# Folding two modulation vectors, and four places in the order of a one-core transformer block

## The chip, the cores and the metric

The kernel runs on one core of a Trainium2 chip. The metric is the device time of one execution in microseconds; lower is better. Profiles come from the hardware profiler, from one execution each.

The engines are named as the profile names them: PE is TensorE's matrix multiplication and PEld its weight load, DVE is VectorE, ACT is ScalarE, POOL is GpSimd, SP is SyncE, which here issues plain DMAs. GpSimd issues the DMAs that add to what they find at their target.

## The reference

One block over `x` of 2048 tokens by 448 channels, all in float32: a linear attention with 16 heads of 28 channels, then a mixer that multiplies across the tokens. Six modulation vectors of 448 values come from the conditioning vector `c`.

```python
mod = (_silu(c) @ w_mod)                 # 6 x 448: sa, ca, ga, sb, cb, gb
h = _layernorm(x) * (1 + ca) + sa
qkv = h @ wqkv
phi = lambda t: where(t > 0, t + 1, exp(t)) + 1e-6
kv, z = phi(k)^T v per head, sum of phi(k) over tokens
o = (phi(q) kv) / (phi(q) z + 1e-6)
x = x + ga * (o @ wo)
h = _layernorm(x) * (1 + cb) + sb
u = gelu(h^T @ w1 + b1)                  # contraction over 2048 tokens, 1792 wide
x = x + gb * (u @ w2 + b2)^T
```

In the code the vectors have numbers: 0 is `sa`, 1 `ca`, 2 `ga`, 3 `sb`, 4 `cb`, 5 `gb`.

## The kernel before, in words

**Two parts for one number.** Matrix products run in the fast 32-bit form, which rounds its operands. So most operands are cut into a high part (a rounded copy, made by ScalarE) and a low part (the rest), and one product becomes three matmuls: high by high, high by low, low by high. `split` (line 78) does it with ScalarE and VectorE. Some low parts are made the other way: ScalarE writes minus the high part, and a DMA of GpSimd adds the full number to it (`w_low_dma`, line 217; `low`, line 399; the second branch of `a_pk_parts`, line 424). A projection of one tile of 128 tokens is 11 matmuls, over four chunks of the 448 channels; the last chunk has 64 channels and holds its high and low part in one tile, so it needs two.

**The stages.** First the modulation vectors 0 and 1 and tile 0. Then a loop over the tiles, one pass for each `t` from 3 to 15 (line 594): TensorE projects the keys of tile `t` (`kp`), transposes tile `t + 1` (`tp`), and adds the outer product of tile `t - 3` (`cacc`, from the parts of phi(k), `pkh` and `pkl`, and of the normalised rows, `xh` and `xl`). The other engines normalise tile `t + 2`, make phi(k) of tile `t`, cut phi(k) of tile `t - 1` into its parts, take the statistics of tile `t + 3` and so on. After the loop the key-value matrices are formed, then come the queries, the residual and the second layer norm (a loop from line 855), the first mixer product (`up`, to line 1163) and the second (`y`, to line 1183), which uses Strassen's seven products on 2 x 2 blocks.

**What sets the order.** Every engine runs its instructions in the order in which the program writes them down; there is no scheduler. So the place of a call in the loop's body is its place in that engine's queue, and an instruction that waits holds up all behind it on its engine. Waits between engines and for buffers are put in from the data each instruction uses. Most tiles share one pool of 76 buffers (`slots`).

**The places the change touches.**

- `project` (line 343) writes down the 11 matmuls of a projection. With `late_low` it sorts them: high parts by high weights first, then low parts, then the low weights, then chunk 3. Only the queries of tile index 1, the second tile, are projected so (line 582). Of their weights' low parts, `wl0_0` comes by DMA (line 541), the others from VectorE.
- Vectors 2 to 5 are summed off the critical start: `mod_part` multiplies 112 rows of `w_mod` by `silu(c)` and adds them up over four pieces on VectorE, so that one tile of 112 rows by 448 is left, whose column sums are the vector. `mod_split` (line 191) cuts it into two tiles, `mod_sum2` (line 196) sums the columns with a matrix of ones: one matmul for the high part (line 199), one for the low part (line 200). `mod_out` copies the result. For vector 2 the four parts are in passes 5 to 8, the split at the end of pass 9, the sum and the copy in pass 10; in passes 11 to 14 the four row groups of `wo` are multiplied by it (line 611). For vector 4 the parts are in passes 11 to 14 (`MOD_AT`), split and sum after the loop (lines 670 and 686).
- `PK_LOW` lists the tiles whose low part of phi(k) VectorE makes, beside `DVE_LOW`. For the others it is ScalarE and GpSimd's DMA.
- `mult7` (line 1014) writes the matmuls of the second mixer product. For the very last product the last `LAST` of 7 row blocks are set aside for `last7` (line 1038), which puts them into a bank of their own, `yl`, with three matmuls of 224 columns for each; VectorE then adds the two halves of the main bank and the closing bank to `x`, and the result is stored.

Of the kernel before, what the change touches and what calls it, by code (L numbers as in the profile page):

```python
# [11 lines left out]
ALU = mybir.AluOpType  # L12
# [3 lines left out]
S, D, F = 2048, 448, 1792  # L16
NT = S // P
NF = F // P
G = 112
# [7 lines left out]
Q_EARLY = (3, 4)  # L27
QLATE = 2
MOD_ACT = (0, 1)
PK_LOW = (9,)  # L30
DVE_LOW = (0, 1, 13, 14, 15)
AHEAD = 8
LAG = 5
LAST = 2
PRE2 = {16: (1, 0), 12: (1, 1), 8: (1, 2), 3: (4, 3), 1: (4, 4)}
MOD_AT = {11: [(4, 0)], 12: [(4, 1)], 13: [(4, 2)], 14: [(4, 3)], 15: [(3, 0), (3, 1)]}
QS = {0: 2, 4: 2}
WARM = 9
ACT_STATS = ()
PRE = 9  # L40
# [7 lines left out]
def block_kernel(ctx: ExitStack, tc: tile.TileContext, x, wqkv, wo, w1, b1, w2, b2, c, wmod, out):  # L48
    nc = tc.nc
# [22 lines left out]
    def moving(new, name, dt=F32R, parts=P):  # L72
        return new(name, dt=dt, parts=parts, w=512)[:, 16:16 + D]

    def bank(name):
        return psum.tile([P, 512], F32, name=name, tag="bank")

    def split(full, hi, lo):
        nc.scalar.activation(hi, full, AF.Copy)  # L79
        nc.vector.tensor_sub(lo, full, hi.bitcast(F32))  # L80
# [4 lines left out]
    ones_r = cst.tile([P, P], F32R, name="ones_r")  # L85
# [55 lines left out]
    def keep_warm(n):  # L141
        for i in range(n):
            nc.tensor.matmul(warm[:, :P], ones, ones, start=True, stop=True)
# [3 lines left out]
    nc.tensor.transpose(ct, c_sb, ident[:4, :4])  # L147
    keep_warm(WARM)

# [7 lines left out]
    mods, macc, part = {}, {}, {}  # L157
# [17 lines left out]
    def mod_part(j, k):  # L175
        if k == 0:
            macc[j] = (tslot if j == 5 else slot)(f"acc{j}", parts=G)
            if j == 5:
                nc.scalar.activation(macc[j], wm[j, 0], AF.Copy, scale=sc[:, 0:1])
            else:  # L180
                nc.vector.tensor_scalar_mul(macc[j], wm[j, 0], sc[:, 0:1])
        else:
            nc.vector.scalar_tensor_tensor(macc[j], wm[j, k], sc[:, k:k + 1], macc[j], op0=ALU.mult, op1=ALU.add)
# [4 lines left out]
        return ps  # L188


    def mod_split(j):
        acc = macc.pop(j)
        macc[j] = (moving(slot, f"mh{j}", parts=G), moving(slot, f"ml{j}", parts=G))
        split(acc, *macc[j])

    def mod_sum2(j):
        ps = bank(f"modp{j}")
        hi, lo = macc.pop(j)
        nc.tensor.matmul(ps[:, :D], ones_r[:G, :], hi, start=True, stop=False)
        nc.tensor.matmul(ps[:, :D], ones_r[:G, :], lo, start=False, stop=True)  # L200
        return ps
# [103 lines left out]
    def a_norm_a(t):  # L305
        h = slot(f"h{t}", 512)
        nc.vector.scalar_tensor_tensor(h[:, :D], X[t], st[t][0], mods[1],
                                       op0=ALU.add if t in ACT_STATS else ALU.subtract, op1=ALU.mult)
        hs[t] = h

    def a_norm_b(t, sa=None):
        h = hs[t]
        nc.vector.scalar_tensor_tensor(h[:, :D], h[:, :D], st.pop(t)[1], mods[0] if sa is None else sa,
                                       op0=ALU.mult, op1=ALU.add)

    def a_dup(t):
        nc.scalar.activation(hs[t][:, D:], hs[t][:, 384:D], AF.Copy)
# [3 lines left out]
    def a_transpose(t):  # L321
        h = hs[t]
        tps[t] = bank(f"tp{t}")
        for ch in range(4):
            nc.tensor.transpose(tps[t][:, ch * P:(ch + 1) * P], h[:, ch * P:(ch + 1) * P], ident)  # L325

    def a_split(t):
        hh = slot(f"hh{t}", 512, F32R)
        hl = slot(f"hl{t}", 512, F32R)
        split(tps.pop(t), hh, hl)  # L330
        heads[t] = (hh, hl)
# [11 lines left out]
    def project(t, j, name, late_low=False):  # L343
        hh, hl = heads[t]
        ps = bank(f"{name}{t}")
        o = ps[:, :D]
        todo = []
        for ch in range(4):
            a, b = (hh, ch, Whi[j, ch]), (hl, ch, Whi[j, ch])
            todo += [a, b] if ch == 3 else [a, (hh, ch, Wlo[j, ch]), b]  # L350
        if late_low:
            ws = [Wlo[j, ch] for ch in range(3)]
            key = lambda m: 3 if m[1] == 3 else 2 if any(m[2] is w for w in ws) else 0 if m[0] is hh else 1
            todo.sort(key=key)
        for n, (a, ch, b) in enumerate(todo):
            nc.tensor.matmul(o, a[:, ch * P:(ch + 1) * P], b, start=(n == 0), stop=(n == 10))  # L356
        return o
# [3 lines left out]
    def a_exp(t, ps):  # L361
        eks[t] = (slot(f"ek{t}"), slot(f"rk{t}"))
        nc.scalar.activation(eks[t][0], ps, AF.Exp)
        nc.scalar.activation(eks[t][1], ps, AF.Relu)
# [20 lines left out]
    def a_q(t):  # L385
        qps[t] = project(t, 0, "qp")
        del heads[t]
# [33 lines left out]
    def a_pk(t, ps):  # L421
        pkf[t] = phi_k(t, ps, tslot if t < 2 else slot)

    def a_pk_parts(t):
        pk = pkf.pop(t)
        hi, lo = moving(slot, f"pkh{t}"), moving(slot, f"pkl{t}")
        nc.scalar.activation(hi, pk, AF.Copy, bias=1e-6)
        if t in DVE_LOW or t in PK_LOW:
            nc.vector.scalar_tensor_tensor(lo, pk, 1e-6, hi.bitcast(F32), op0=ALU.add, op1=ALU.subtract)
# [14 lines left out]
    def a_outer(t):  # L444
        if not cacc:
            cacc.extend(bank(f"cacc{ch}") for ch in range(4))
        xh, xl = xss.pop(t)
        kh, kl = pks.pop(t)
        for ch in range(4):
            s = slice(ch * P, (ch + 1) * P)  # L450
            todo = [(xh, kh), (xh, kl)] + ([(xl, kh)] if ch < 3 else [])
            for i, (a, b) in enumerate(todo):
                nc.tensor.matmul(cacc[ch][:, :D], a[:, s], b, start=(t == 0 and i == 0),  # L453
                                 stop=(t == NT - 1 and i == len(todo) - 1))
# [137 lines left out]
    wo_sb = []  # L592
    late = [t for t in range(KV_LAG, NT) if t not in Q_EARLY]
    for t in range(3, NT):
        kp = project(t, 1, "kp")
        if t + 1 < NT:
            a_transpose(t + 1)
        a_outer(t - KV_LAG)
        if t in Q_EARLY:
            a_q(t)  # L600
        if t == 10:
            mp = mod_sum2(2)
        if t + 1 < NT:
            a_split(t + 1)
        if t + 2 < NT:
            a_norm_a(t + 2)

        for j, i in MOD_AT.get(t, ()):
            mod_part(j, i)
        if 11 <= t < 15:  # L610
            nc.vector.tensor_mul(wo_sb[t - 11], wo_sb[t - 11], mods[2][:G])
        a_exp(t, kp)
        if t + 2 < NT:
            a_norm_b(t + 2)
        a_pk(t, kp)
        a_phi_q()
        a_pk_parts(t - 1)
        if t + 3 < NT:
            a_stats(t + 3)
        if t + 2 < NT:  # L620
            a_dup(t + 2)
        if t == 3:
            a_high(3)
            a_high(4)
        if t + 2 < NT:
            a_high(t + 2)
        if t == 10:
            mod_out(2, mp)
        if t + 4 < NT:
            load_x(t + 4)  # L630
        if 5 <= t < 9:
            mod_part(2, t - 5)
        if t == 9:
            mod_split(2)
        if 5 <= t <= 5 + QLATE:
            phi_q_sum(t - 5)
        if t in (10, 11):
            load_mod(14 - t)
        if t == 4:
            for g in range(4):  # L640
                w = tslot(f"wo{g}", parts=G)
                nc.sync.dma_start(w, wo[g * G:(g + 1) * G, :])
                wo_sb.append(w)
            load_qkv(2, tslot)
            b1c = cst.tile([P, NF], F32, name="b1c")
            nc.sync.dma_start(b1c, b1.rearrange("(k p) -> p k", p=P))
            b2c = cst.tile([P, NT], F32, name="b2c")
            nc.sync.dma_start(b2c, b2.rearrange("(k p) -> p k", p=P))
        load_to(PRE_LOAD.get(t, 0))
# [38 lines left out]
    for ch in range(4):  # L688
        for g in range(4):
            s = slice(g * G, (g + 1) * G)  # L690
            nc.tensor.matmul(kvb[:G, s], raw_w[2, ch][:, s], csum[ch][:, s], start=(ch == 0 and g == 0),  # L691
                             stop=(ch == 3), skip_group_check=True)
# [162 lines left out]
    for i in range(NT + LAG):  # L855
# [6 lines left out]
        if 0 <= i - 1 < NT:  # L862
            b_out(i - 1)
        nq = min(len(late), QS.get(i, 1))
        for _ in range(nq):
            a_q(late.pop(0))
        t = i - LAG
# [146 lines left out]
    def mult7(q, m, r0, r1):  # L1014
# [6 lines left out]
        for r in range(r0, r1):  # L1021
            (h, l), i = hilo[q, m][r // 4], r % 4
            w, wh = uops[b, r]
            s = slice(i * P, (i + 1) * P)
            if (q, m) == (NP - 1, 6) and r >= PAIRS - LAST:
                last.append((h[:, s], l[:, s], w))
                continue
            nc.tensor.matmul(ps[:, :D], h[:, s], w, start=opens and r == r0, stop=False, skip_group_check=True)  # L1028
            nc.tensor.matmul(ps[:, :HD], l[:, s], wh, start=False,  # L1029
                             stop=closes and r == PAIRS - 1 - (LAST if (q, m) == (NP - 1, 6) else 0),  # L1030
                             skip_group_check=True)
# [6 lines left out]
    def last7():  # L1038
        x = X[NT - 1][:, :HD]
        ps = bank("yl")[:, :HD]  # L1040
        for i, (h, l, w) in enumerate(last):
            for n, (a, b) in enumerate(((h, w[:, :HD]), (h, w[:, HD:]), (l, w[:, :HD]))):
                nc.tensor.matmul(ps, a, b, start=i + n == 0, stop=n == 2 and i == LAST - 1)
        for s in (acc2[NP - 1, 0][:, :HD], acc2[NP - 1, 0][:, HD:D], ps):
# [97 lines left out]
    for o0, n in W1G[1:]:  # L1142
# [5 lines left out]
        for r in range(first, NT):  # L1148
# [4 lines left out]
            if xleft and k % 2:  # L1153
                t = xleft.pop(0)
# [11 lines left out]
    for q, m, r0, r1 in order:  # L1166
        if jobs:
            jobs.pop(0)()
        while xleft:
            t = xleft.pop(0)  # L1170
# [41 lines left out]
```

## Time and profile before

| | |
|---|---|
| median of 3 runs | 440.61 us (440.5 to 441.14) |
| the profiled execution | 440.77 us |
| its span, first to last instruction | 439.1 us |
| granted TensorE clock | 1.000 |
| busy: DVE | 365.1 us (83%) |
| busy: ACT | 266.9 us (61%) |
| busy: POOL | 119.3 us (27%) |

Times in the profile count from the span's start. Busy times are the union of an engine's instructions. Matmuls are pipelined: the rows give each some 0.36 us for 448 columns, but the next one starts 0.20 us later, so their starts are what to compare. In the chain of work that ended last each line is start, length, and engine with tile and line; in a timeline a row is start, length, engine, line, operation, tiles, shapes and count, and in brackets how long the engine was idle before it and what ended that. Weight loads (PEld) run ahead of the matmuls; a matmul that must wait for its stationary operand shows as an idle PEld.

### The profile page before, as it was taken

The numbers are of one execution on the slowest core, as the hardware profiler recorded it, in microseconds if no ns is written. First come the engines' busy times: TensorE is split into PE (matmuls) and PEld (weight loads), VectorE is DVE, ScalarE is ACT, GpSimd is POOL, SyncE is SP. The second block draws the span as 40 slices with busy tenths as digits, with TensorE's granted clock in tenths as the row PEclk, the third lists the DMA queues.
The fourth block names the chain that finished last, engine by engine and source line by source line (L and its number), as shares of the span: only waits on it lengthen the run. The fifth ranks groups of instructions, "written<-read, shape, count | busy, mean of one in ns | idle before, by whom it ended". The sixth has DMA issues, their size and how long they took to land.

```text
span 439.1 us, 7288 instructions
## 1 busy us (share of the span) xinstructions
PE 433.9 (99%) x2394; PEld 402.4 (92%) x2394; DVE 365.1 (83%) x792; ACT 266.9 (61%) x570; POOL 119.3 (27%) x196
## 2 busy tenths in 40 slices
PE   8999999999999999999999999999999999999996
PEld 7689999999899999999999999999999999999996
DVE  5996898988898999997469586439999998898894
ACT  3778877655657777776766254236675555655550
POOL 2205775520024455664300000010112230231110
PEclk9999999999999999999999999999999999999999
DMA  8987999993441224222427546476667977977531
GB/s 233 303 213 117 181 197 230 221 258 102 138 100 26 47 47 123 50 50 60 132 69 237 177 143 186 131 194 187 151 143 191 177 172 176 188 161 208 75 52 34
DMA packets 65022, 64.51 MB, mean 147 GB/s; under 512 B 8472, under 2 KB 56792, under 8 KB 64984
## 3 DMA queue, kind: packets, MB, share of 16 engines
q1 hardware_dynamic: 54608, 47.62, 36.8%
q0 software_dynamic: 10368, 16.42, 23.8%
q8 instruction: 19, 0.31, 0.3%
q14 instruction: 19, 0.16, 0.1%
q10 hardware_dynamic: 8, 0.00, 0.0%
HBM read 41.88 MB, written 7.34 MB: 112 GB/s over the span
## 4 chain that ended last, share of the span: by engine, by line
PE 95%; DMA 3%; DVE 1%; ACT 0%; issue 0%; SPq 0%; DVEq 0%
PE y L1028 19%; PE up L829 10%; PE up L828 10%; PE up L830 10%; PE y L1029 9%; PE op L778 8%; PE cacc L453 8%; PE qp L356 7%; PE kp L356 7%; DMA wl<-wr 2%; PE tq L758 2%; PE tp L325 1%; DMA wm<-in_w_mod_dram 1%; PE kvb L691 1%; PE wp L846 1%; PE colp L475 0%
## 5 line engine op out<-in xcount | busy, mean ns | idle before, releaser
L829 PE MATMUL up<-h2l,ph 128*128 128x448 f32 x224 | 81.3, 363 | 0.0
L828 PE MATMUL up<-h2h,ph 128*128 128x448 f32 x224 | 81.2, 362 | 0.0
L830 PE MATMUL up<-h2h,pl 128*128 128x448 f32 x224 | 80.7, 360 | 0.0
L988 POOL DMA_DIRECT2D a<-a x16 | 14.1, 948 | 145.5 <-DMA a<-in_B_w_dram 97.8
L828 PEld LDWEIGHTS up<-h2h,ph 128*128 128x128 f32 x224 | 42.0, 188 | 3.3
L830 PEld LDWEIGHTS up<-h2h,pl 128*128 128x128 f32 x224 | 41.9, 187 | 3.0
L829 PEld LDWEIGHTS up<-h2l,ph 128*128 128x128 f32 x224 | 42.0, 188 | 2.1
L80 DVE TENSOR_TENSOR pl<-pr,ph 128x512 fp32r<-128x512 f32 x48 | 32.3, 686 | 11.5 <-ACT ph L79 8.6
L79 ACT ACTIVATE ph<-pr 128x512 fp32r<-128x512 f32 x48 | 29.1, 627 | 17.8 <-PE up L829 7.4
L1050 ACT ACTIVATE cc<-y 128x448 f32<-128x448 f32 x24 | 13.0, 544 | 22.9 <-PE y L1029 22.9
L453 PE MATMUL cacc<-pkh,xh 128*128 128x448 f32 x64 | 24.3, 379 | 0.0
L453 PE MATMUL cacc<-pkl,xh 128*128 128x448 f32 x64 | 23.2, 363 | 0.0
L778 PE MATMUL op<-oh,pth 128*128 128x448 f32 x60 | 23.0, 383 | 0.0
L1071 POOL DMA_DIRECT2D out_dram<-yt x14 | 12.9, 921 | 34.9 <-DVE yt L1057 25.4
L778 PE MATMUL op<-oh,ptl 128*128 128x448 f32 x60 | 21.7, 362 | 0.0
L356 PE MATMUL qp<-wh,hh 128*128 128x448 f32 x60 | 21.6, 365 | 0.0
L356 PE MATMUL qp<-wh,hl 128*128 128x448 f32 x60 | 21.4, 362 | 0.0
L356 PE MATMUL kp<-wh,hl 128*128 128x448 f32 x56 | 20.3, 363 | 0.0
L356 PE MATMUL kp<-wh,hh 128*128 128x448 f32 x56 | 20.2, 362 | 0.0
L736 POOL TENSOR_SCALAR den<-den 128x16 f32<-128x16 f32 x16 | 8.6, 536 | 39.2 <-DVE den L733 39.1
L763 ACT ACTIVATE pth<-tq 128x512 fp32r<-128x512 f32 (+1 forms) x16 | 9.6, 599 | 15.7 <-PE tq L758 15.6
L302 POOL TENSOR_TENSOR rs<-ve,mhalf 128x1 f32<-128x1 f32 x16 | 13.9, 869 | 18.8 <-DVE ve L300 18.5
(234 smaller groups left out, 1356.9 us busy)
## 6 DMA issues: line engine op xcount, KB each, us to landing
pr<-in_B_w_dram SPq DMA_DIRECT2D x56, 256.0 KB, 2.9
a<-in_B_w_dram SPq DMA_DIRECT2D x32, 256.0 KB, 4.3
a<-in_B_w_dram SPq DMA_DIRECT2D x32, 192.0 KB, 4.2
wm<-in_w_mod_dram SPq DMA_DIRECT2D x24, 196.0 KB, 4.9
x<-in_A_x_dram SPq DMA_DIRECT2D x16, 224.0 KB, 4.0
out_dram<-x SPq DMA_DIRECT2D x14, 224.0 KB, 2.0
out_dram<-yt POOLq DMA_DIRECT2D x14, 224.0 KB, 4.5
pk<-pk POOLq DMA_DIRECT2D x12, 224.0 KB, 4.7
```

The costliest lines, as they stand in the source:

```text
L79: nc.scalar.activation(hi, full, AF.Copy)
L80: nc.vector.tensor_sub(lo, full, hi.bitcast(F32))
L302: nc.gpsimd.tensor_tensor(rs, ve, mhalf[:, 0:1], op=ALU.pow)
L356: nc.tensor.matmul(o, a[:, ch * P:(ch + 1) * P], b, start=(n == 0), stop=(n == 10))
L453: nc.tensor.matmul(cacc[ch][:, :D], a[:, s], b, start=(t == 0 and i == 0), stop=(t == NT - 1 and i == len(todo) - 1))
L778: nc.tensor.matmul(opb[t][:, :D], a[:, g * P:(g + 1) * P], b, start=(n == 0), stop=(n == len(todo) - 1))
L828: nc.tensor.matmul(ps[:, :D], hi[:, sl], mh, start=first, stop=False)
L829: nc.tensor.matmul(ps[:, :D], hi[:, sl], ml, start=False, stop=False)
L830: nc.tensor.matmul(ps[:, :D], lo[:, sl], mh, start=False, stop=last)
L988: nc.gpsimd.dma_start(w, a, accum_op=ALU.add)
L1028: nc.tensor.matmul(ps[:, :D], h[:, s], w, start=opens and r == r0, stop=False, skip_group_check=True)
L1029: nc.tensor.matmul(ps[:, :HD], l[:, s], wh, start=False, stop=closes and r == PAIRS - 1 - (LAST if (q, m) == (NP - 1, 6) else 0), skip_gro ...
```

## The change

Five edits.

1. Vectors 2 and 4 are folded. When the 112-row tile is complete, a DMA of GpSimd with add puts rows 64 to 111 onto rows 0 to 47 of the same tile (`fold`). The split then takes 64 rows, and writes the high part to rows 0 to 63 and the low part to rows 64 to 127 of one tile, so that one matmul with 128 rows of ones sums both.
2. To make room for the fold of vector 2, it is issued at the end of pass 8, the split moves to the end of pass 10, sum and copy to pass 11, and the multiplications of `wo` to passes 12 to 15. The fold of vector 4 is issued in pass 14, right after its last part, ahead of that pass's other work on GpSimd.
3. In the late order of the second tile's queries, the product with `wl0_0` stands last, behind the other two low parts and chunk 3.
4. Tile 7's low part of phi(k) is made by VectorE.
5. `LAST` is 3 instead of 2.

```diff
-PK_LOW = (9,)
+PK_LOW = (7, 9)
-LAST = 2
+LAST = 3
+FOLDED = (2, 4)
...
+    def fold(j):
+        nc.gpsimd.dma_start(macc[j][:G - 64], macc[j][64:], accum_op=ALU.add)
+
     def mod_split(j):
         acc = macc.pop(j)
+        if j in FOLDED:
+            macc[j] = moving(slot, f"mb{j}")
+            split(acc[:64], macc[j][:64], macc[j][64:])
+            return
         macc[j] = (moving(slot, f"mh{j}", parts=G), moving(slot, f"ml{j}", parts=G))
...
     def mod_sum2(j):
         ps = bank(f"modp{j}")
+        if j in FOLDED:
+            nc.tensor.matmul(ps[:, :D], ones_r, macc.pop(j), start=True, stop=True)
+            return ps
...
-            key = lambda m: 3 if m[1] == 3 else 2 if any(m[2] is w for w in ws) else 0 if m[0] is hh else 1
+            key = lambda m: 3 if m[1] == 3 else 4 if m[2] is ws[0] else 2 if any(m[2] is w for w in ws) else 0 if m[0] is hh else 1
...
-        if t == 10:
+        if t == 11:
             mp = mod_sum2(2)
...
-        if 11 <= t < 15:
-            nc.vector.tensor_mul(wo_sb[t - 11], wo_sb[t - 11], mods[2][:G])
+        if t == 14:
+            fold(4)
+        if 12 <= t < 16:
+            nc.vector.tensor_mul(wo_sb[t - 12], wo_sb[t - 12], mods[2][:G])
...
-        if t == 10:
+        if t == 11:
             mod_out(2, mp)
...
         if 5 <= t < 9:
             mod_part(2, t - 5)
-        if t == 9:
+        if t == 8:
+            fold(2)
+        if t == 10:
             mod_split(2)
```

## The prediction

> **What bounds the kernel now.** I read the page first, then the chain of work that ended last, then TensorE's and its weight loads' timeline around each place that the diff touches.
>
> ```profile
> span 439.1 us, 7288 instructions
> PE 95%; DMA 3%; DVE 1%; ACT 0%; issue 0%; SPq 0%; DVEq 0%
> ...
> 17.43 8.12 DMA wl<-wr
> 25.60 3.48 PE qp L356 x16
> ```
>
> The chain is TensorE for 95% of 439.1 us. The only long piece of another kind behind the first microseconds is the DMA of `wl0_0`, 8.12 us, which ends at 25.55; TensorE takes up at 25.60 and is the chain from there to the last adds. So a change pays here in two coins only: matmuls that are no longer there, and holes in TensorE's row. Work on other engines costs nothing until it makes such a hole. The profiled execution took 440.77 us (its span and 1.67 around it), 0.16 over the median of the runs, 440.61. Some 0.2% (0.88 us) is about what a measurement of this kernel can tell from no change.
>
> **Part 1: the low part of the query weights last.** The query projection of tile index 1 (the second tile) waits for `wl0_0`, the one low part that comes by DMA.
>
> ```profile
> 24.75 0.77 PE L356 MATMUL qp<-wh,hl 128*128 128x448 f32 x3
> 25.60 0.88 PE L356 MATMUL qp<-wl,hh 128*128 128x448 f32 x3
> 26.31 0.36 PE L356 MATMUL qp<-wh,hh 128*128 128x448 f32 x1
> 26.51 0.36 PE L356 MATMUL qp<-wh,hl 128*128 128x448 f32 x1
> ...
> 25.60 0.50 PEld L356 LDWEIGHTS qp<-wl,hh 128*128 128x128 f32 x3 [0.45 <-DMA wl<-wr]
> ...
> 22.87 0.62 DVE L213 TENSOR_TENSOR wl<-wr,wh 128x448 fp32r<-128x448 f32 x1
> ```
>
> Undisturbed, matmuls start 0.20 apart (26.31, 26.51). Three from 24.75 would hand over at 25.35; the next starts at 25.60: 0.25 lost. From there three should take 0.60, but the next follows at 26.31: 0.11 more while the row restarts. That is 0.36. In the new order the two low parts that VectorE makes come next, then the two products of chunk 3, then `wl0_0`: four matmuls, 0.80, sooner than they would wait. VectorE's last low part ends at 23.49 and the one of chunk 3 follows it directly, so those four find their data. `wl0_0` is then wanted at 25.35 + 0.80 = 26.15, its weights some 0.2 before, 25.95; it lands at 25.55. Margin 0.4. Gain 0.36; bounds 0 (the DMA lands 0.8 later than here) and 0.36. Nothing is issued differently. What is late next: nothing near, as every matmul behind it runs at its 0.20.
>
> **Part 2: the two folded vectors.**
>
> ```profile
> 72.38 0.20 PE modp L199
> 72.58 0.21 PE modp L200
> ...
> 108.22 0.20 PE modp L200
> ```
>
> Each sum is now two matmuls of 112 rows; folded, it is one of 128 rows. One piece of 0.21 and one of 0.20 leave the chain: 0.41. That 128 rows take no longer than 112 is in the rows: 0.20 for the modulation sums and 0.20 between the projections' matmuls, which have 128. The Trainium skill (TensorE: Matmul & The Clock Gate, Back-to-back issue gap) gives a sustained 131 ns per matmul of 512 columns; by that figure the two would be worth 0.26 at most, and the whole sum below 0.86. The trace does not agree: its 448 columns take 200 ns, and I go by the trace.
>
> The price is on GpSimd and VectorE. `fold` is a DMA with add on GpSimd's queue, 48 rows of 448 floats (84 KB). The fold of vector 2 comes at the end of tile 8's pass, behind `xl`; the split moves from the end of pass 9 to the end of pass 10, and sum and evacuation from pass 10 to 11.
>
> ```profile
> 66.85 0.88 POOL L404 DMA_DIRECT2D xl<-h  x1 [0.89 <-ACT rk L364]
> 70.37 0.87 POOL L432 DMA_DIRECT2D pkl<-pk  x1 [2.64 <-ACT mh L79]
> ...
> 72.03 0.89 POOL L302 TENSOR_TENSOR rs<-ve,mhalf 128x1 f32<-128x1 f32 x1
> ...
> 74.61 0.85 POOL L438 DMA_DIRECT2D pk<-pk  x1 [0.34 <-issue]
> ...
> 72.95 0.68 DVE L313 SCALAR_TENSOR_TENSOR h<-h,rs,mod 128x448 f32<-128x448 f32 x1 [0.91 <-POOL rs L302]
> ...
> 73.67 0.26 ACT L317 ACTIVATE h<-h 128x64 f32<-128x64 f32 x1 [1.61 <-DVE h L313]
> ...
> 74.84 0.60 PE L325 MATMUL tp<-ident,h 128*128 128x128 f32 x4
> ...
> 74.86 0.53 ACT L161 ACTIVATE mod<-modp 128x448 f32<-128x448 f32 x1
> ...
> pk<-pk POOLq DMA_DIRECT2D x12, 224.0 KB, 4.7
> wl<-wr POOLq DMA_DIRECT2D x1, 224.0 KB, 8.1
> ol<-wpl SPq DMA_DIRECT2D x1, 84.0 KB, 2.2
> ```
>
> GpSimd would issue the fold at about 67.7 (66.85 + 0.88). Queued behind it are `pkl` of tile 8, the running sum `pk`, then the power that gives tile 12 its `rs`, then the next `xl`. Its landing lies between 2.2 (the same size on SP's queue) and 8.1 (the slowest accumulating DMA); nearest is the accumulating `pk`, 4.7, so 72.4. The split takes the place of `mod` on ScalarE, 74.86, so it finds its data; at 8.1 (75.8) ScalarE would be held 0.9 and with it the split of the next transposes, which TensorE reads some 2.2 after making them. I take nothing, and keep 0.9 for the range of the rivals. The Trainium skill (DMA: Bandwidth & Descriptors, Anatomy of one DMA) puts a GpSimd DMA at about 2.0 us plus bytes over 436 GB/s: by that, an estimate, 2.2 here. The trace does not agree for this queue: 224 KB would be 2.5 by it and show 4.7 and 8.1.
>
> VectorE's half of the split moves into pass 10, where it idles 0.91 for GpSimd's `rs` (the row at 72.95); it lasts about 0.6, like the subtraction of this width at 22.87. Moving the multiplications of the output weights one pass later changes when, not how many. The fold of vector 4 falls late in the stage.
>
> ```profile
> POOL den L736 <- DVE den L733: 39.1, 14, 23.1
> ```
>
> After its last accumulates there GpSimd idles 23.1 us, and the sum of vector 4 stands at 108, so that fold is free.
>
> **Part 3: tile 7's low part by VectorE.**
>
> ```profile
> 65.24 2.21 PE cacc L453 x11
> ...
> 70.09 2.29 PE cacc L453 x11
> ...
> 63.37 0.86 POOL L432 DMA_DIRECT2D pkl<-pk  x1 [0.57 <-ACT pkl L431]
> ...
> DMA to landing us min/median/max: 3.2/4.1/6.7
> ```
>
> The outer product at 70.09 is tile 7's; it is 0.08 longer than its neighbour. Its low part was issued at 63.37 and fits the one that took 6.7: landed at 70.07, just as it was wanted. On VectorE it is there long before: gain 0.08 (bounds 0 and 0.08). It costs VectorE one operation of 0.62, takes one off ScalarE, and takes one 224 KB DMA off the queue in which the 84 KB fold now stands. I set the two against each other: the queue comes out no slower.
>
> **Part 4: the longer closing bank.**
>
> ```profile
> 433.90 0.82 DVE L1060 TENSOR_TENSOR xb<-cc,xb 128x224 f32<-128x224 f32 x2
> ...
> 434.66 0.11 PE y L1029
> ...
> 434.80 0.40 DVE xb L1045
> ...
> 435.23 0.40 DVE xb L1045
> ...
> 435.72 0.39 DVE xb L1045
> ...
> 435.16 0.28 PE L1043 MATMUL yl<-ut,a22l 128*128 128x224 f32 x1
> ...
> 321.59 0.68 DVE L80 TENSOR_TENSOR ut<-ta,ut 128x224 fp32r<-128x224 f32 x2
> ```
>
> The first closing add follows the main bank's end (434.77) by 0.03; the second and third follow their predecessors, while the closing bank was ready at 435.44. Closing the main bank one row block earlier frees it about 0.31 sooner, at 434.46, but VectorE is then in the adds of 433.90, whose second ends at 434.72 and so began near 434.32 (0.40 each). Two independent operations of this width overlap, 0.30 from start to start (0.68 less 0.38 for a pair), so the first closing add could start at 434.32 + 0.30 = 434.62; I take 434.64. The third then starts at 435.56. TensorE's closing bank has one block more, about 0.02 longer, and is ready at 435.50. Gain 0.16; if the adds do not overlap, 0.06.
>
> **The sum.** 0.36 + 0.41 + 0.08 + 0.16 = 1.01. Of the profiled execution that makes 439.76, of the median **439.60**. Its own range is a gain of 0.7 to 1.05, 439.55 to 439.9.
>
> **Rivals.**
>
> *GpSimd's queue (slower).* If the fold is not paid for by the DMA that leaves, `rs` of tile 12 comes late. Before, the last piece of tile 12's rows is ready at 73.93 (73.67 + 0.26) and the transposes start at 74.84: 0.91 spare. In the changed kernel their turn comes 0.36 + 0.08 + 0.41 sooner, the latter because the sums move behind them: spare 0.06. So every later microsecond of `rs` is one of TensorE. The four steps from 66.85 to 74.61 average 1.94 per DMA, the first is 3.52. A fold that costs a step like this first one puts TensorE back 3.46, net +2.45: 443.1; with the mean step 441.5. It decides from `rs` starting later than 73.1, 1.07 over now. For it: GpSimd stood 2.64 before the very next DMA. Against: 224 KB leave this stretch and 84 KB come.
>
> *VectorE becomes the bound.*
>
> ```profile
> 80.90:85.90 5.00, 4.93 (x12) 1.00 0.95 191
> ...
> 83.29 0.68 DVE L313 SCALAR_TENSOR_TENSOR h<-h,rs,mod 128x448 f32<-128x448 f32 x1
> ...
> 84.34 0.56 PEld L325 LDWEIGHTS tp<-ident,h 128*128 128x128 f32 x4
> ```
>
> In tile 12's pass VectorE is busy 4.93 of 5.00. It finishes tile 14's rows at 83.97, 0.37 before they are loaded; TensorE will come 0.65 sooner by then. If VectorE comes no sooner, 0.28 is given back there; with adds that don't overlap at the end 0.10 more: gain 0.63, 439.98. Against: the pass before loses one multiplication of the output weights.
>
> *A later wait takes it.*
>
> ```profile
> PEld y L1028 <- DVE ut L80: 0.2, 1, 0.2
> ```
>
> TensorE waits 0.2 for VectorE near 322, where VectorE is in one unbroken run. If that run does not start earlier with TensorE, the hole grows by all that was won before, and only the end's 0.16 is left: 440.45. Against: VectorE's work there is made from TensorE's own results.
>
> *It doesn't do what it says.* If `wl0_0` lands 0.8 later once more, part 1 gives nothing: gain 0.65, 439.96. Nothing in the diff delays it.
>
> **How the numbers follow.** Forecast 0.60, of which 0.10 lies below 0.88 by its own bounds; GpSimd's queue 0.09; VectorE 0.18; the later wait 0.08; the late landing 0.05. Faster by over 0.2%: 0.50. Within: 0.10 + 0.18 + 0.08 + 0.05 = 0.41. Slower: 0.09. The range runs from 439.25 (the sum, the wait near 322 gone as well, and the 0.11 by which the lowest run lies under the median) to 440.7 (the later wait's case with as much scatter above it); it leaves out the queue's case.
>
> **What would show it.** Right: no wait of the query projection on `wl`, the outer product of tile 7 at 2.21, one `modp` matmul for vectors 2 and 4, the first closing add near 0.15 ahead of now relative to TensorE's end, and TensorE's row otherwise unbroken. Wrong: a wait of `tp` on `h` near 74 or 84, a `pkl` wait at tile 8's outer product, a split of vector 2 held by the fold's DMA, or a wait near 322 that has grown past 0.2.

## The result and the profile after

| | before | after |
|---|---|---|
| median on record before the prediction | 440.61 us | |
| medians side by side on one chip, 9 runs each | 441.14 us | 439.75 us (439.66 to 440.84) |
| the profiled execution | 440.77 us | 439.79 us |
| its span | 439.1 us | 438.1 us |

The ratio of the times is 0.9976, 95% interval 0.9964 to 0.9987: faster by 0.24%. Forecast were 439.60 for the median and 439.76 for a profiled execution.

First the page of the changed kernel, its head and the shares of the chain of work that ended last.

```profile
span 438.1 us, 7287 instructions
PE 433.5 (99%) x2393; PEld 402.4 (92%) x2393; DVE 365.7 (83%) x793; ACT 266.3 (61%) x569; POOL 120.1 (27%) x197
...
PE 97%; DMA 1%; DVE 1%; SPq 0%; issue 0%; DVEq 0%
```

The chain is TensorE's for 97% where it was 95%: the 8.12 us of `wl<-wr` are no longer on it. Then pieces of that chain at the five places (start, length, engine, tile, line).

```profile
24.34 4.41 PE qp L367 x22
...
69.78 2.21 PE cacc L464 x11
...
76.85 0.20 PE modp L207
...
107.43 0.20 PE modp L207
...
433.51 0.39 DVE xb L1075
433.91 0.31 DVE xb L1060
434.24 0.40 DVE xb L1060
...
434.74 0.39 DVE xb L1060
```

The queries of the second and the third tile run 22 matmuls without a break. Tile 7's outer product takes 2.21, as its neighbours do. Each folded vector is one matmul of 0.20. At the end the closing adds begin while TensorE still works. The chain counts a piece only from the end of the one before it, so the start of the first closing add is read from VectorE's timeline, and that of the last `yl` matmul from TensorE's:

```profile
433.83 0.81 DVE L1060 TENSOR_TENSOR xb<-y,xb 128x224 f32<-128x224 f32 x2
...
434.38 0.27 PE L1058 MATMUL yl<-ut,a22l 128*128 128x224 f32 x1
```

The last add (434.74) begins 0.36 behind the last `yl` matmul, where it was 0.56 (435.16 and 435.72).

To compare executions that start up at different speeds I take two stretches between starts in TensorE's timeline: **stretch A** from the first query matmul of the second tile to the first matmul of the key-value matrices (`kvb`), and the **tail** from the last `yl` matmul to the last closing add.

| kernel | A begins | A ends | A | tail |
|---|---|---|---|---|
| before | 24.05 | 108.26 | 84.21 | 0.56 |
| after | 24.10 | 107.47 | 83.37 | 0.36 |

A is 0.84 shorter, the tail 0.20. The start-up took 0.05 longer and the rest is unchanged to 0.01, which together is the span's 0.98.

### The profile page after: what moved, and what is told of

Read it like the earlier page. It is cut to its first block, busy times and chain, and to the rows that moved or that the text cites. A ratio compares the mean times of both kernels' runs of the same rounds, so it can differ in the third digit from the quotient of the medians.

```text
span 438.1 us, 7287 instructions
## 1 busy us (share of the span) xinstructions
PE 433.5 (99%) x2393; PEld 402.4 (92%) x2393; DVE 365.7 (83%) x793; ACT 266.3 (61%) x569; POOL 120.1 (27%) x197
## 4 chain that ended last, share of the span: by engine, by line
PE 97%; DMA 1%; DVE 1%; SPq 0%; issue 0%; DVEq 0%
PE y L1043 19%; PE up L844 10%; PE up L843 10%; PE up L845 10%; PE y L1044 9%; PE op L793 8%; PE cacc L464 8%; PE qp L367 8%; PE kp L367 7%; PE tq L773 2%; PE tp L336 1%; DMA wm<-in_w_mod_dram 1%; PE kvb L706 1%; PE wp L861 1%; PE qp L513 1%; PE kp L513 1%
## 5 line engine op out<-in xcount | busy, mean ns | idle before, releaser
L960 DVE TENSOR_TENSOR u<-u,mod 128x448 f32<-128x448 f32 x14 | 8.7, 619 | 11.9 <-ACT u L959 11.6
```

## The experiments

Each experiment is the changed kernel with one edit, except two that are the old kernel with one part of the change. Beside the theory of the prediction (each part pays its own term) stood a rival: that the two DMA waits, at 25 and 70, aren't two terms, because what TensorE saves at the first it waits at the second.

The times alone don't separate these kernels from the changed one. Its ratio to the kernel before was 0.9976 and, on another chip, 0.9985; the four kernels with one part taken back lie between 0.9981 and 0.9990. So the sizes below are those of stretches in one profiled execution of each kernel.

**The old order of the queries, everything else new.**

```diff
-key = lambda m: 3 if m[1] == 3 else 4 if m[2] is ws[0] else 2 if any(m[2] is w for w in ws) else 0 if m[0] is hh else 1
+key = lambda m: 3 if m[1] == 3 else 2 if any(m[2] is w for w in ws) else 0 if m[0] is hh else 1
```

> The changed kernel with the old order of the second tile's queries (the product with wl0_0 in seventh place of eleven). Theory A (each edit is worth its own hole in TensorE's row): the hole depends on when the DMA of wl0_0 lands. Its data are wanted at about 25.35; landing at 25.55 as in the profile of before leaves a hole of 0.36 and a span of 438.45; landing at 24.09 as in the profile of the changed kernel leaves none and a span of 438.1. Rival B (the landing is no matter of chance, the old order always loses 0.3 to 0.4): a hole of 0.3 to 0.4 whatever the execution, and about 0.36 us more than the changed kernel in the median.

440.15 us against 440.91 for the kernel before, ratio 0.9981 (0.9972 to 0.9990). A is 83.36, no longer than in the changed kernel. Below are the old order's timeline of TensorE at the place and, from the view of the tile, how long the low part's DMA took.

```profile
24.88 0.76 PE L367 MATMUL qp<-wh,hl 128*128 128x448 f32 x3
25.48 0.76 PE L367 MATMUL qp<-wl,hh 128*128 128x448 f32 x3
```

```profile
DMA to landing us min/median/max: 7.2/7.2/7.2
```

The first product with `wl0_0` follows 0.20 after the last of the three before it: no hole, in the old order. The DMA took 7.2 here (8.1 in the profile before) and landed at 24.82, ahead of its use. So in this execution part 1 is worth nothing. In the changed kernel's profiled execution it earned nothing either: there `wl0_0` landed at 24.09, and the old order loads these weights 1.10 behind A's beginning, at 25.20.

**Tile 7's low part by DMA again, everything else new.**

```diff
-PK_LOW = (7, 9)
+PK_LOW = (9,)
```

> The changed kernel with tile 7's low part of phi(k) by ScalarE and GpSimd's DMA again, so that this DMA and the fold of vector 2 both stand in GpSimd's queue. Theory A (terms are independent): the outer product of tile 7 is 0.08 longer, span 438.2. Rival C (tile 7's edit pays for the fold): GpSimd's power for tile 12 starts 1.9 to 3.5 us later than its 70.52, at 72.4 to 74.0; the transposes of tile 12 (first weight load near 74.0) then wait 0.7 to 2.3, span 438.8 to 440.4, and tile 8's low part, landing at 72.97 now, comes after the 74.6 at which it is wanted.

440.32 us, ratio 0.9985 (0.9976 to 0.9994), span 438.7. A is 83.76, 0.39 more than in the changed kernel. The chain there, and below it the weight load that waited:

```profile
63.25 7.03 DMA pkl<-pk
...
70.32 2.28 PE cacc L464 x10
```

```profile
69.70 0.19 PEld L464 LDWEIGHTS cacc<-pkh,xh 128*128 128x128 f32 x1
70.31 0.19 PEld L464 LDWEIGHTS cacc<-pkl,xh 128*128 128x128 f32 x1 [0.43 <-DMA pkl<-pk]
```

The part landed at 70.27. In the kernel before it landed at 70.06, and TensorE, delayed by the wait at 25, lost 0.08 on it. Without that wait it loses 0.39. GpSimd's row of the same kernel shows the fold beside this DMA:

```profile
67.13 0.88 POOL L415 DMA_DIRECT2D xl<-h  x1 [1.23 <-ACT pkh L438]
67.72 1.14 POOL L193 DMA_DIRECT2D acc<-acc  x1
70.58 0.91 POOL L443 DMA_DIRECT2D pkl<-pk  x1 [1.72 <-issue]
71.73 0.85 POOL L449 DMA_DIRECT2D pk<-pk  x1 [0.24 <-issue]
72.29 0.87 POOL L313 TENSOR_TENSOR rs<-ve,mhalf 128x1 f32<-128x1 f32 x1
```

With the fold in the queue and no DMA taken out, `rs` of tile 12 starts at 72.29: 0.26 later than before (72.03), not the 1.94 to 3.52 that the rival on GpSimd's queue charged. Even the 0.26 is not the fold's: A began 0.25 later in this execution (24.30 and 24.05). The last piece of tile 12's rows is ready at 74.18 and the transposes begin at 74.64, so TensorE does not notice. Without the hole at 70 the transposes would have come near 74.25, though, and the spare would have been 0.07.

**The closing bank as before, everything else new.**

```diff
-LAST = 3
+LAST = 2
```

> The changed kernel with two row blocks in the closing bank. Theory A: the first closing add again follows the main bank's end, and the time from TensorE's last matmul to the last add's start goes from 0.36 (434.38 to 434.74) back to 0.56 (435.16 to 435.72): 0.19 longer, span 438.3. Rival (VectorE's earlier adds set it): no difference.

440.12 us, ratio 0.9983 (0.9975 to 0.9992). The tail is 0.56 (434.23 to 434.79), as in the kernel before. The chain's last lines:

```profile
433.84 0.02 issue
433.87 0.40 DVE xb L1060
...
434.29 0.40 DVE xb L1060
...
434.79 0.39 DVE xb L1060
```

The first closing add waits for TensorE's main bank and begins at 433.87, 0.36 before the last `yl` matmul starts. In the changed kernel it begins 0.55 before it (433.83, 434.38), 0.32 behind the add ahead of it (433.51); the second add follows 0.41 later there and 0.42 here. So the whole of the gain is the first add's earlier start. The longer bank shortens the tail by 0.20.

**No folds, all else new** (the split, sum and multiplications stay in their new passes).

```diff
-FOLDED = (2, 4)
+FOLDED = ()
...
-            fold(4)
...
-            fold(2)
```

> The changed kernel with no vector folded and no fold issued, but sum and split of vector 2 still one pass later. Theory A: two matmuls more in TensorE's row, one of 0.20 in pass 11 and one of 0.20 before the key-value matrices, nothing else; span 438.5, about 0.41 us over the changed kernel. Rival (the folds' DMAs cost something elsewhere that hides part of the gain): less than 0.3 us over the changed kernel.

440.43 us, ratio 0.9990 (0.9982 to 0.9999), span 438.9. A is 83.77, 0.40 more than with the folds. The chain shows where:

```profile
77.24 0.20 PE modp L210
77.44 0.21 PE modp L211
...
108.02 0.21 PE modp L210
108.23 0.20 PE modp L211
```

Two pieces more, of 0.20 each, and nothing else. The folds are worth the two matmuls.

**The changed kernel once more, on another chip.**

> The changed kernel once more, beside the kernel before on this chip, as the base for the three others of this call. No hole in TensorE's row between 21 and 320, span about 438.1, ratio to before 0.9976 as measured.

440.01 us against 440.74, ratio 0.9985 (0.9976 to 0.9993). A is 83.35, the tail 0.36.

**The order of the queries alone, on the kernel before** (the edit of the first experiment, the other way round).

> The kernel before with nothing but the new order of the second tile's queries. Theory D (the two DMA holes are one: the low part of tile 7 lands by GpSimd's queue at a time that TensorE does not move, 70.06 and 70.27 in the two profiles seen, so what is won at 25 is lost there): no hole at 25, a hole of 0.4 to 0.5 at tile 7's outer product, span 439.0 to 439.1, no gain against the kernel before. Theory A (each edit is worth its own hole): a hole of 0.08 there, and a gain of 0.36 wherever the old order would have waited.

440.78 us against 440.74, ratio 0.9997 (0.9988 to 1.0005). A is 84.29. Two kernels that sum each vector in two matmuls and have no hole need 83.77 (no folds, above, and tile 7's part alone, below), so 0.52 are lost here. TensorE has no hole at 25, and one at 70; its weight loads there, and at the transposes of tiles 14 and 15:

```profile
69.68 0.19 PEld L453 LDWEIGHTS cacc<-pkh,xh 128*128 128x128 f32 x1
70.20 0.19 PEld L453 LDWEIGHTS cacc<-pkl,xh 128*128 128x128 f32 x1 [0.33 <-DMA pkl<-pk]
...
84.65 0.43 PEld L325 LDWEIGHTS tp<-ident,h 128*128 128x128 f32 x4 [0.21 <-DVE h L313]
...
89.65 0.43 PEld L325 LDWEIGHTS tp<-ident,h 128*128 128x128 f32 x4 [0.30 <-DVE h L313]
```

`pkl` of tile 7 landed at 70.16, close to the 70.06 of before and the 70.27 of the second experiment, and cost 0.33. The other 0.2 was lost at the two transposes: `rs` of tile 14 began at 82.64, 0.53 later behind A's beginning than before (81.89), VectorE waited 0.43 for it, and TensorE for VectorE's rows. `wl0_0` landed at 25.30, just before the old order would have loaded it (25.37), so in this execution that order would not have waited either. The run shows that without a wait at 25 there is one at 70; part 1 alone gains nothing in the times.

**Tile 7's part alone, on the kernel before.**

```diff
-PK_LOW = (9,)
+PK_LOW = (7, 9)
```

> The kernel before with nothing but tile 7's low part by VectorE. Theory D: with the later hole gone, the one at 25 shows in full when wl0_0 lands late (0.36 at a landing of 25.55, none at 24.1); gain against before 0.08 when it is late, 0.4 to 0.5 when it is early, so about 0.1 to 0.4 in the median. Theory A: a gain of 0.08, not to be seen in times.

440.71 us against 440.74, ratio 1.0001 (0.9992 to 1.0011). In its profiled execution A is 83.77: no hole at 70, and none at 25 either, since `wl0_0` came in time. That is the 0.44 of both waits with one edit, span 438.7. The times don't bear it out: 0.44 would be a ratio of 0.9990, just outside the interval. One profiled execution says what happened in it, not how often.

**All four late vectors folded** (3 and 5 as well, the split of vector 5 one pass later).

```diff
-FOLDED = (2, 4)
+FOLDED = (2, 3, 4, 5)
...
+    fold(3)
...
-        mp = mod_sum2(5) if i == NT else None
+        mp = mod_sum2(5) if i == NT + 1 else None
...
+            fold(5)
+        if i == NT:
             mod_split(5)
```

> The changed kernel with vectors 3 and 5 folded too: fold 3 right behind its last part after the loop, fold 5 behind its last part with split, sum and copy of vector 5 one pass later. Theory A: two matmuls less, 0.41 under the changed kernel, span 437.7, if no new hole opens. Rival E (a fold needs cover): the sum of vector 5 now stands beside eight banks in use, four of each pass of the first mixer product, so TensorE waits for the copy to free one, a hole of 0.3 to 1 near 206; or the split of vector 3 waits for its fold and holds the copies of the key-value matrices, a hole near 108. Then no gain, or slower by up to 0.6 than the changed kernel.

443.28 us against 440.74, ratio 1.0047 (1.0031 to 1.0064): slower. The chain around 206:

```profile
204.57 0.58 ACT h2h L838
205.14 0.65 ACT sqa L296 x2
205.80 0.65 ACT sqb L296 x2
206.45 0.47 ACT mb L80
...
206.95 0.63 DVE mb L81
...
207.62 0.47 PE modp L207
```

TensorE has a hole of 2.12 before this `modp`. The fold had landed at 204.42, so it isn't what was waited for: the split, one pass later, stands on ScalarE behind that pass's norm and squares and comes to VectorE and TensorE only then. The expectation had the place right, but took the wait for one on a bank. The profiled execution took 442.02; the median lies 1.26 above it, and what the other runs lost beyond this hole no trace shows. The fold of vector 3 did its part: the stretch from A's beginning to the first matmul of `up` shrank by 0.22.

**Vector 3 folded too, vector 5 not** (the `fold(3)` line of the edit above, with `FOLDED = (2, 3, 4)`).

> The changed kernel with vector 3 folded as well (its fold right behind its last part after the loop), vector 5 as before. Theory A: one matmul less behind the key-value matrices, 0.20 under the changed kernel from the second tile's queries to the first mixer product (123.69 in its profile, so 123.48), no new hole; ratio to before about 0.0005 under the changed kernel's. Rival E (the fold lacks cover): the split of vector 3 waits for the fold on ScalarE and holds zb or the copies of the key-value matrices, a hole near 107.

439.61 us (439.34 to 440.16) against 440.77, ratio 0.9974 (0.9963 to 0.9984), span 437.9. No new hole; the way to `up` is 0.22 shorter (123.47 from A's beginning where the changed kernel needs 123.69). ScalarE does wait 1.48 for this fold, but TensorE does not wait for what stands behind it. It beats both kernels in the trace; the times of the changed kernel and this one can't be told apart.

**The fold without its pass of cover: the split of vector 2 one pass sooner.**

```diff
-        if t == 10:
+        if t == 9:
             mod_split(2)
```

> The changed kernel with the split of vector 2 back at the end of pass 9, so that it follows its fold by one pass less; the sum stays in pass 11. Theory F (the moved pass is the fold's cover): the fold lands near 71.5, ScalarE reaches the split near 68.9 and is held 2.6; the split of tile 11's transposes starts near 72 instead of 69.8, VectorE's half ends near 73.3, and the key projection of tile 11 (72.0, third matmul 72.4) waits about 1. Span 439.1. Rival (the 2.2 between transposes and projection swallow it): no hole over 0.3.

441.67 us in its one run, span 439.9. First ScalarE's timeline, then the totals of TensorE's weight loads' waits:

```profile
68.22 0.53 ACT L414 ACTIVATE xl<-xh 128x384 fp32r<-128x384 f32 x1
71.89 0.58 ACT L80 ACTIVATE mb<-acc 64x448 fp32r<-64x448 f32 x1 [3.15 <-DMA acc<-acc]
72.38 0.57 ACT L80 ACTIVATE hh<-tp 128x512 fp32r<-128x512 f32 x1
```

```profile
PEld kp L367 <- ACT hh L80: 1.7, 1, 1.7
...
PEld kp L367 <- DVE hl L81: 0.6, 1, 0.6
```

The split waits 3.15 for the fold, issued at 66.42 and landed at 71.87. Behind it on ScalarE stands `hh`, the high part of the next tile's transposes, and TensorE loses 2.09 in all. The expectation was about half of that; the direction and the place hold.

**`wl0_0` issued later, with a closing bank of 4.** Two questions in one kernel, since they lie far apart.

```diff
-    w_low_dma(0, 0)
...
     a_dup(2)
+    w_low_dma(0, 0)
...
-LAST = 3
+LAST = 4
```

> The changed kernel with the low part wl0_0 written down later on ScalarE (behind tile 2's duplicate, about 1.5 us), so that its DMA lands later, and, at the other end of the run, with four row blocks in the closing bank. New order of the second tile's queries: wanted at about 26.1 (0.80 later than in the old one); landing at 25.5 to 26.5 gives a hole of 0 to 0.5. At the end: the time from TensorE's last matmul to the last add's start. Theory (VectorE's earlier adds set the first closing add now): no gain, 0.34 to 0.36 from a TensorE row 0.02 longer. Rival: another 0.15 to 0.2.

439.85 us in its one run, span 438.2. The DMA was issued at 19.26 instead of 17.4 and landed at 25.27; no hole. The tail is 0.34 (434.46 to 434.80), against 0.36 with three blocks: no further gain, as VectorE's adds are now one chain. The last `yl` matmul ends near 434.73 (0.27 long) and the second add at 434.70, so the last add has TensorE and VectorE to wait for at about the same time.

**The same delay with the old order of the queries** (`LAST` is 3).

> The changed kernel with wl0_0 written down later in the same way and the old order of the second tile's queries. If the order is worth what the prediction said when the DMA is late, the hole here is landing less 25.35 plus 0.11 (0.3 to 1.3), which is 0.5 to 0.8 more than beside the new order, and the span is longer by as much, since no later DMA hole is left to swallow it. Rival: the hole is swallowed further on, spans alike.

439.95 us in its one run, span 438.2. Inconclusive. The kernel was to make the low part late and so show what the order is worth. TensorE's timeline, and the time of the DMA:

```profile
24.95 0.76 PE L367 MATMUL qp<-wh,hl 128*128 128x448 f32 x3
25.55 0.76 PE L367 MATMUL qp<-wl,hh 128*128 128x448 f32 x3
```

```profile
DMA to landing us min/median/max: 4.9/4.9/4.9
```

Issued 1.7 later, the DMA took 4.9 instead of 6.0 to 8.5 and landed at 23.98, sooner than in any other profile. Nothing was late.

## Why the prediction was right, and where it was not

The sum held: 1.01 forecast, 0.98 in the profiled execution (439.79 where 439.76 stood). On the other chip the ratio makes the gain 0.66. Its four terms did not all hold, and that two of them came out as a sum was luck in part.

**The folds: right.** 0.41 forecast, 0.40 between the kernels without and with them. The Trainium skill (TensorE: Matmul & The Clock Gate, Back-to-back issue gap) gives a sustained 131 ns for 512 columns; by it the folds would have been worth 0.26 at most. The runs decide for the row: 0.20 per matmul of 448 columns. The cover held as well: the fold of vector 2 was issued at 67.13 and landed at 71.46, in 4.3 where 4.7 was taken, ahead of its split at 73.74.

**The closing bank: right.** The first closing add was to start 0.32 behind the add ahead of it (434.32, 434.64), and does (433.51, 433.83). The tail shrank by 0.20; the stretch from the first `kvb` matmul to the last `yl` matmul is 0.01 longer (326.90 and 326.91, up to 326.93 in the other kernels with three blocks), so the net is 0.17 to 0.19 where 0.16 was forecast.

**The two DMA waits: right as a sum, wrong as two terms.** 0.36 and 0.08 were priced from one execution, each as if the other stayed. But the low part of tile 7 landed 46.01, 45.89 and 45.97 behind A's beginning in the three executions that make it by DMA, the first with the wait at 25 and the others without. Its issue did follow TensorE (39.32, then 38.96 and 38.95), but the transfer took 6.7, then 6.9 and 7.0. Why it took longer is not shown, and three executions do not rule out chance. The step that failed is "bounds 0 and 0.08" for tile 7: with no wait at 25 its hole is 0.39 in A, and 0.33 in the kernel with part 1 alone. So part 1 alone gained nothing, and part 3 takes 0.39 in the changed kernel and the 0.44 of both waits on the kernel before. The changed kernel has neither wait, which is why the sum came out.

**The query order's own value: seen in the landings, not in the times.** The prediction took the landing at 25.55 for the rule and allowed for a later one only; at an earlier one neither order waits. Over the fourteen profiles `wl0_0` landed between 0.27 ahead of A's beginning and 1.81 behind it (1.50 in the kernel before). The old order loads these weights 1.10 behind A's beginning, the new one 1.90. Of the ten profiles in the new order seven have the landing between the two, at 1.12 to 1.81, and none has a hole. By the prediction's own sum (the landing less 1.25, plus 0.11, which makes before's 0.36) four of them, at 1.39 to 1.81, would have cost the old order an estimated 0.25 to 0.67. That is an estimate: of the four profiled executions in the old order only that of the kernel before has the hole, the attempt to make the landing late failed, and the times show no difference between the orders. The margin of 0.4 shrank to 0.09 in the changed kernel's execution on the other chip.

**The rivals.** GpSimd's queue: its condition was that the fold isn't paid for, and its price a step of 1.94 to 3.52. With the condition made true the price was 0.01 (`rs` 47.99 behind A's beginning, 47.98 before). It did not fail for lack of a narrow margin, which was 0.07 where 0.06 was forecast, but in its price. With tile 7's DMA gone `rs` comes 46.42 behind A's beginning with the folds and 46.34 without them. So in the changed kernel the queue gains 1.51 instead (`rs` at 70.52 for 72.03):

```profile
66.55 0.85 POOL L415 DMA_DIRECT2D xl<-h  x1
67.13 1.11 POOL L193 DMA_DIRECT2D acc<-acc  x1
68.29 0.89 POOL L443 DMA_DIRECT2D pkl<-pk  x1
69.95 0.86 POOL L449 DMA_DIRECT2D pk<-pk  x1 [0.77 <-DVE xh L423]
70.52 0.88 POOL L313 TENSOR_TENSOR rs<-ve,mhalf 128x1 f32<-128x1 f32 x1
```

VectorE: it ends tile 14's rows at 83.37 (83.97 before), and the weights of the transposes are loaded at 83.76 (84.34), so the spare is 0.39 where it was 0.37; it moves with TensorE. The wait that this rival feared appears only in the kernel with part 1 alone, where `rs` of tile 14 came late. The later wait: one line of the weight loads' waits,

```profile
PEld y L1043 <- DVE ut L81: 0.2, 1, 0.2
```

is as long as before. It moved with TensorE too.

## What to carry to other kernels

Waits of one engine for transfers that land at times of their own are not terms to add up: what is saved at the first is waited for at the second, so price the last one with the earlier ones already gone, and look at more than one execution before a DMA's landing is taken for fixed. A fold that halves the matmuls of a small sum is worth exactly those matmuls, and only while everything behind its DMA on the splitting engine has a pass of slack: 2.1 us went where that pass was missing, and 2.1 where the split itself was moved behind other work. A closing bank pays until the adds behind it are one chain, here at three blocks.

## What the runs showed of the hardware

**GpSimd's DMAs have places.** Their issues in the kernel before stand 0.31 behind a landing again and again: `pkl` at 70.37 after 70.06, `pk` at 71.47 after 71.16, `xl` at 73.40 after 73.09. At each of these issues three DMAs of 128 rows are then under way. With the fold of 48 rows among them there are four (in the changed kernel those issued at 62.83, 66.55, 67.13 and 68.29, of which the first landed at 69.64), and the next `pk` is issued at 69.95, again 0.31 behind it. So the fold cost the queue no place, and a large DMA taken out frees one. What is counted, the trace does not say.

**A DMA's time varies.** The same 224 KB for `wl0_0` took 4.9 to 8.5 us over the fourteen profiles, least in the two kernels that issue it later (6.0 and 4.9). The 84 KB of a fold took 4.3 to 5.6 near 67, 3.6 to 4.8 near 92 and 2.8 at 202. What sets the time is not shown. The Trainium skill (DMA: Bandwidth & Descriptors, Anatomy of one DMA) gives 2.0 us plus bytes over 436 GB/s, for the fold an estimated 2.2; every fold here took longer.

**Executions differ at the start.** The first query matmul of the second tile started between 23.79 and 24.50 over the kernels profiled, none of which differs ahead of it by more than one DMA's place. That is 0.7 us of scatter under an effect of 1.0, which is why stretches are compared here and not spans alone.
